# One unit of the next-to-last feed-forward job moved behind the last step of a two-layer recurrent transformer kernel

## The chip, the cores and the metric

The kernel runs on one core of one Trainium2 chip. The metric is the device time of one execution in microseconds (us). Engines are named as in the profile: PE is TensorE's matmul, PEld its weight load, DVE VectorE, ACT ScalarE, POOL GpSimd, SP SyncE, which issues most of the DMAs.

## The reference

Two layers over the same weights. Each layer is an attention block whose segments are chained by a memory, and a gated feed-forward block. All inputs are bf16; S = 2048 tokens, D = 576, 32 heads of 128, segments of 32 tokens, a memory of 8 tokens, F = 4608.

```python
def attention(x, mem, Wq, Wk, Wv, Wo):           # x: (1, 2048, 576)
    for s in range(64):                           # segments of 32 tokens
        h = concatenate([mem, x[:, 32*s:32*s+32]])          # 40 rows
        q, k, v = (einsum('btd,dhe->bhte', h, W) for W in (Wq, Wk, Wv))
        p = softmax(where(mask, q @ k.T * 128**-0.5, -1e9))
        o = einsum('bhte,hed->btd', p @ v, Wo)
        mem = o[:, :8]                            # the next segment needs it
        outs.append(o[:, 8:])
    return concatenate(outs)
def feed_forward(x, w1, w3, w2):
    return (silu(x @ w1) * (x @ w3)) @ w2

x = A_x
for _ in range(2):
    x = x + attention(layernorm(x), A_mem0, Wq, Wk, Wv, Wo)
    x = x + feed_forward(layernorm(x), w1, w3, w2)
```

## The kernel before

**Steps.** The memory chains the segments, so the kernel walks through them in 72 steps: in step t it computes segment t of the first layer (t below 64) and segment t - 8 of the second (t from 8 on). In steps 8 to 63 both layers' 40 rows go through the same matmuls as 80 columns; from step 64 on only the second layer is left. A step has eight groups of Q/K projections (letters Q for the full 128-row part, q for the 64-row rest), four of scores (S), transposes of the probabilities (T on TensorE where one layer is left, a DMA transpose into PTS where there are two), P x V (P), output projections (O, o), and V projections (V, v, X, x or G, g).

**Jobs.** After every fourth step 128 finished tokens of each layer go to a feed-forward job: POST (p) transposes them back and adds them to the residual XR, a layer norm follows on DVE and POOL, its transposes (n) go to PSUM, and `xtb_write` copies them into the tile XTB, 128 columns for each of the job's two groups of tokens (`bi`, the half). Then come nine units (`pp`), each with two pairs of up matmuls (`ffn_up`: F the full part, f the 64-row rest, 2 x 128 features of w1 and of w3), tanh on ACT, two multiplications on DVE into HTT, and then down matmuls (`ffn_down`, W or w) whose result two DVE instructions add to XR. The up weights of a pair (W13, four DMAs) have two slots, the down weights (W2C, one DMA a pair) two, so a load waits until an earlier unit's matmuls have freed its slot.

**The end.** Job 16 (group 14 of the second layer) runs beside steps 68 to 71, job 17 (group 15) after step 71. Each has one group of 128 tokens. Job 17 finds the weights of unit 8 still in the W13 and W2C slots, where job 16 leaves them (`kept`). For units 0 to 7 the attention weights are no longer needed: four chunks of up weights (1024 features, 2.4 MB each) are loaded into the tile W, and four of down weights (1.2 MB each) into WV (`tail_load`). An up chunk waits for the Q/K projections of step 71 that read its columns, a down chunk for that step's V projections (`last_reads`). Units 0 and 1 use chunk 0, units 2 and 3 chunk 1, and so on. Ahead of job 17's transposes, `ln_tr` issues ten matmuls on data that nothing reads (`warm`).

**Order.** `make_nodes` makes a list of nodes, each with its engine, an estimated duration, its dependencies and the slots that it takes and frees. The order on TensorE is written out as letters: `ORDER = FIRST + FOUR * 11 + LAST`, where FIRST covers steps 0 to 15, each FOUR four steps, and LAST steps 60 to 71. Nodes of a kind are taken in the order in which they were made. `plan` runs through that list with the estimated times and puts the other engines' nodes, SP's DMAs among them, in the order of the earliest planned start, by `prio` among those that could start; a node marked AD goes to ACT or DVE, whichever could start it first. Each engine then executes its list in order. All helpers record under one line each: L594 the matmuls, L597 ACT, L600 DVE, L603 SP's loads and stores, L1024 the DMA transposes, L1015 POOL's clearing of PB.

Of the kernel before, what the change touches and what calls it, by code (L numbers as in the profile page):

```python
# [7 lines left out]
BF = mybir.dt.bfloat16  # L8
# [187 lines left out]
def ewh(*ns):  # L196
# [15 lines left out]
    "vQQQQqfqWSFSFfqqqQQwWQFPfqfSFwQOPSWFoFPffOOWPwOoooFqqfQQWQSqqqQQaSbQQqgqqGSQgPGSGPGggOPOwOPoooOo"  # L212
)
LAST = (
    "QqqqpQQQSnpQQqqqVvSSnQFqfFqPfQOwSPWfFPOOoFfooFPWOoFffqqQQwQSFffqqFQQQgqqwWSGSQPFQqfgqGSWFPGfggGPOOOPwOooooFqqfqQ"
    "QQQfqWSFSvQQqqVwSFqfqQPQFSWPwOOPffFOWPwOooooFfqqQQQQqfqWSwVSFFvfqqQQQqqSPQWSOPVvPwOObPoooxOoXVppvqqQQQSqqQQqqnnS"
    "QQFTSqfQPqFSTOfPFTOPWTOPwOooooFqffqQQQSQqqVvSFTQqfqQQSFqfqwPQWTOSPFTOffPFTOPwOWooooFfqqQQQwSQqqfvxXVWSFFQfqqTQPw"
    "WTFSQQffqqFPSOTwWFPffOTFPWOOwooooFvqqfQQQSwQqqVSWFQfqfqFQQSTWPQqqOTSPoTOPwOToboPxOoXqqqQQQpSvVqqqQQnSQFSfTQFqqfP"
    "QOSTFfPowTOPfFTOPFOooowQqqfqQFSQQvqqfVSQFfqQQTSFqfqwPQTFPSOTXfxPOTOPwOooooFVvqfQQqqQSQqqqfQSQFTSQPqqQwOFToSfPFTO"
    "fPwTOPFOooofQQqqqqQSQQSvqqQVwTQSQqfqfPSTOPoFOTFPTOPwOooopfFFfnwFffffFFFwFfFwffFFwfffFFwFwfffFFFwffFFwfffFFww"  # L220
)
ORDER = FIRST + FOUR * 11 + LAST

# [5 lines left out]
    ustep, mode_pen, hor, wait, bulk, ff_split, last_win, tail_at = 0.0315, 0.1194, 0.0162, 0.141, 0.02, False, 2.5, -1.5  # L229


def make_nodes(em, nseg, pools, o=Opt, dma_bw=230e3, load_bw=400e3):

    ngrp = nseg // 4
    nodes = []
# [20 lines left out]
    def load(name, nbytes, prio, fn, deps=()):  # L256
        return node("DMA", nbytes / load_bw, fn, deps=deps, prio=prio, name=name, lat=2.0)
# [97 lines left out]
    def step(t):  # L355
# [17 lines left out]
        for g in range(NG):  # L373
# [79 lines left out]
    last_up = []  # L453
    last_reads = [], []
    kept = {}

    def job(j):

        ents = [(0, j)] if 0 <= j < ngrp else []
        if 0 <= j - 2 < ngrp:  # L460
            ents.append((1, j - 2))
# [8 lines left out]
        for (bi, g) in reversed(ents):  # L470
            pa = post(bi, g)
            wr += ln_nodes("F", xr[g], Slot("xn"), [pa], s0, [((lambda bi: lambda b: em.xtb_write(bi, b))(bi), cost, prev_ff)], last)
        mm = (128 * ne / 2.4 + 2.5) / 1000
        w2_last = {}
        tail = None
        if last:
            v_done, qk_done = last_reads
            tail = []
            for i in range(4):
                parts = [(0, 9 * 1024, qk_done[4 * i:4 * i + 4]), (1, 8 * 576, v_done)]  # L480
                tail += [[load("tail", kb(128, c), s0 + o.tail_at + 0.01 * i, em.tail_load(i, what), deps=dep) for what, c, dep in parts]] * 2

        npp = NPR // 2
        for at, pp in enumerate([npp - 1] + list(range(npp - 1)) if last else range(npp)):
            mids, w2s, htts, lds = [], [], [], []
            stays = last and pp == npp - 1
            for pr_ in (2 * pp, 2 * pp + 1):
                prio = s0 + o.ff + (o.win if s0 + 4 < nst else o.last_win) * (2 * at + pr_ % 2) / NPR
                if stays:
                    w13, w2 = kept[pr_]  # L490
                    ld = []
                    w2s.append(w2)
                elif last:
                    w13 = w2 = None
                    ld = tail[pp]
                else:
                    keep = s0 < nst <= s0 + 4 and pp == npp - 1
                    w13, w2 = Slot("w13", users=2 + keep), Slot("w2", users=ne + keep)
                    kept[pr_] = w13, w2
                    ld = [node("DMA", kb(1152, 256) / dma_bw, em.load_w13(pr_, w13), prio=prio - 1, acq=[w13], lat=2.0, name="W13")]  # L500
                    lds.append(node("DMA", kb(256, 576) / dma_bw, em.load_w2(pr_, w2), prio=prio - 0.99, acq=[w2], lat=2.0, name="W2l"))
                    w2s.append(w2)
                b = banks()
                htt = Slot("htt", users=ne)
                rel13 = [w13] if w13 else []
                fm = node("PE", 16 * mm, em.ffn_up(ents, pr_, w13, b, last and not stays, False), deps=wr + ld, prio=prio, mode="full/col",
                          acq=b + [htt], rel=rel13, name="FF")
                ff = node("PE", 2 * mm, em.ffn_up(ents, pr_, w13, b, last and not stays, True), deps=wr + ld, prio=prio + o.fft, mode="row",
                          acq=b + [htt], rel=rel13, name="FFt")
                a = node("ACT", actc(256 * ne), em.ffn_tanh(ents, b, htt), deps=[fm, ff], prio=prio - 0.5, name="tanh")  # L510
                c = node("DVE", 2 * dve(256 * ne) + 0.13, em.ffn_mul(ents, b, htt), deps=[a], prio=prio - 0.5, rel=b, name="mul")
                last_up[:] = [fm, ff]
                mids.append(c)
                htts.append(htt)
            for (bi, g) in ents:
                b = banks()
                d = node("PE", 8 * 0.1225, em.ffn_down(bi, pp, htts, w2s, b, last and not stays), deps=mids + lds, prio=prio + o.w2,
                         mode="full/col", acq=b, rel=htts + w2s, name="W2b" if bi else "W2")
                es = [node("DVE", dve(288), em.ffn_add(g, h, xr[g], b[h]), deps=[d], prio=prio + o.w2, rel=[b[h]], name="W2a")
                      for h in (0, 1)]  # L520
                w2_last[bi] = es
        for (bi, g) in ents:
            if bi == 0:
                ht_set(1, g, ln_nodes("L1", xr[g], Slot("xn"), w2_last[0], s0 + LAG - 4.2, ht_writes(1, g)))
            else:
                xn = Slot("xn")
                c = node("ACT", actc(576), em.fin_cast(xr[g], xn), deps=w2_last[1], prio=s0 + LAG - 4.2, acq=[xn], rel=[xr[g]], name="fin")
                node("SWD", 1.0, em.store(g, xn, last), deps=[c], prio=s0 + LAG - 4.2, rel=[xn], lat=3.0, name="store")

    def x_in(g):  # L530
        xn = Slot("xn")
# [39 lines left out]
class Emitter:  # L571
# [574 lines left out]


    def span(self, ents):
        bis = [bi for bi, _ in ents]
        return min(bis) * P, (max(bis) + 1) * P  # L1150

    def ffn_up(self, ents, pr, w13, b, last, tail):

        def f(n):
            lo, hi = self.span(ents)
            W = self.tail_w[pr][0] if last else self.T.W13[:, w13.i]
            first = self.begin(b)
            for fb in range(2):
                fs = slice(fb * P, (fb + 1) * P)
                os_ = slice(fb * 2 * P + lo, fb * 2 * P + hi)  # L1160
                for r in (0, 1):
                    if tail:
                        rr = slice(r * R64, (r + 1) * R64)
                        self.mm(self.bk(b[r])[:, os_], W[rr, 8, fs], self.T.XTB[rr, 4, lo:hi], first and fb == 0, fb == 1,
                                tile_position=(r * R64, 0))
# [52 lines left out]
def kernel(  # L1218
# [62 lines left out]
    T.M0 = T.XTB[:].rearrange("p a b -> p (a b)")[:, 0:D]  # L1281

    T.banks = [pp.tile([P, 512], F32, name=f"bank{i}") for i in range(pools["bank"])]

# [59 lines left out]
```

## Time and profile before

| What | Value |
|---|---|
| median of 3 runs | 2660.19 us (2660.15 to 2664.9) |
| profiled execution | 2656.83 us |
| its span, first to last instruction | 2654.8 us, mean granted clock 0.994 |
| PE busy | 2575.9 us, 97% of the span |
| DVE, ACT busy | 77%, 46% |
| chain that ended last | PE 83%, DMA 8%, DVE 5% |
| DMA | 373.21 MB, mean 141 GB/s |

The profile is of one execution; the times stated from it are us after its first instruction. Busy times of PE are modelled at the matmuls' ends. "PE <- X" in a list of waits is idle time of TensorE that X ended; "issue" is idle time that no semaphore ended. SPq rows are the times that SP took to issue a DMA, not its transfer. Step 71 begins at 2578.9 us, its POST matmuls (after the wait for YTS) at 2608.2, and the last store is issued at 2651.5.

### The profile page before, as it was taken

The numbers are of one execution on the slowest core, as the hardware profiler recorded it, in microseconds if no ns is written. First come the engines' busy times: TensorE is split into PE (matmuls) and PEld (weight loads), VectorE is DVE, ScalarE is ACT, GpSimd is POOL, SyncE is SP. The second block draws the span as 40 slices with busy tenths as digits, with TensorE's granted clock in tenths as the row PEclk, the third lists the DMA queues.
The fourth block names the chain that finished last, engine by engine and source line by source line (L and its number), as shares of the span: only waits on it lengthen the run. The fifth ranks groups of instructions, "written<-read, shape, count | busy, mean of one in ns | idle before, by whom it ended". The sixth has DMA issues, their size and how long they took to land.

```text
span 2654.8 us, 132820 instructions
## 1 busy us (share of the span) xinstructions
PE 2575.9 (97%) x58915; PEld 2224.6 (84%) x58915; DVE 2040.2 (77%) x5241; ACT 1229.2 (46%) x3648; POOL 334.7 (13%) x399
## 2 busy tenths in 40 slices
PE   5999999999999999999999999999999999999998
PEld 4788888888888888888888888888888887888876
DVE  4787777787787777877778787778877877877766
ACT  2555454444445444444445444454544434454553
POOL 1111110110111011010101111010111101111110
PEclk8999999999999999999999999999999999999999
DMA  9064845565565546456554655545455565544466
GB/s 322 4 185 122 195 107 142 123 147 138 126 153 116 136 118 165 126 135 165 109 132 116 153 135 134 157 119 140 109 141 143 126 156 107 136 116 137 130 181 222
DMA packets 686033, 373.21 MB, mean 141 GB/s; under 512 B 233896, under 2 KB 675632, under 8 KB 684816
## 3 DMA queue, kind: packets, MB, share of 16 engines
q1 hardware_dynamic: 681920, 356.84, 53.3%
q8 instruction: 460, 7.54, 1.2%
q0 software_dynamic: 3024, 6.93, 0.9%
q10 hardware_dynamic: 512, 0.94, 0.2%
q14 instruction: 117, 0.96, 0.1%
HBM read 308.49 MB, written 2.36 MB: 117 GB/s over the span
## 4 chain that ended last, share of the span: by engine, by line
PE 83%; DMA 8%; DVE 5%; SPq 2%; ACT 1%; issue 1%; POOL 0%; ACTq 0%; DVEq 0%; POOLq 0%
PE bank L594 83%; DMA PTS<-PB 5%; SPq L603 1%; DVE STAT L600 1%; DVE V L600 1%; DVE HTT L600 1%; DVE PB L600 1%; DMA W<-in_B_w_dram 1%; DMA W<-in_A_Wk_dram 1%; DVE SME L600 1%; ACT V L597 1%; DMA WV<-in_A_Wv_dram 0%; DVE XR L600 0%; DMA W2C<-in_B_w_dram 0%; POOL PB L1015 0%
## 5 line engine op out<-in xcount | busy, mean ns | idle before, releaser
L594 PEld LDWEIGHTS <-W 128*128 128x128 bf16 (+2 forms) x31824 | 1253.7, 100 | 138.5 <-issue 66.4
L594 PE MATMUL bank<-HT,W 128*128 128x80 bf16 (+3 forms) x23040 | 803.2, 197 | 20.6 <-DMA W<-in_A_Wk_dram 8.7
L594 PE MATMUL bank<-XTB,W 128*64 128x256 bf16 (+5 forms) x8784 | 666.6, 263 | 5.8 <-DMA W<-in_B_w_dram 5.5
L1015 POOL MEMSET PB<- 128x1024 bf16 x288 | 273.9, 951 | 1949.4 <-DMA PTS<-PB 1294.9
L597 ACT ACTIVATE QKT<-bank 128x256 bf16<-128x256 f32 (+4 forms) x1557 | 358.8, 315 | 303.9 <-PE bank L594 295.3
L594 PE MATMUL bank<-OT,WO 128*128 128x80 bf16 (+3 forms) x11520 | 412.1, 198 | 1.1 <-ACT OT L597 0.6
L594 PEld LDWEIGHTS <-WO 128*128 128x128 bf16 (+1 forms) x11520 | 383.7, 102 | 25.9 <-issue 13.5
L597 ACT ACTIVATE V<-bank 64x512 bf16<-64x512 f32 (+1 forms) x582 | 328.6, 584 | 127.3 <-PE bank L594 120.1
L594 PE MATMUL bank<-WV,HT 128*64 128x512 bf16 (+3 forms) x3960 | 376.0, 386 | 1.1 <-DVE HT L600 0.7
L594 PE MATMUL bank<-W2C,HTT 128*64 128x288 bf16 (+1 forms) x3088 | 320.0, 287 | 0.7 <-DMA W2C<-in_B_w_dram 0.5
L597 ACT ACTIVATE HTT<-bank 128x512 bf16<-128x512 f32 (+1 forms) x324 | 175.9, 551 | 273.4 <-PE bank L594 271.8
L600 DVE TENSOR_REDUCE STAT<-SME 104x8 f32<-104x320 f32 (+1 forms) x576 | 273.5, 475 | 16.9 <-ACT SME L597 10.5
L597 ACT ACTIVATE OT<-bank 128x320 bf16<-128x320 f32 (+1 forms) x380 | 142.8, 402 | 306.3 <-PE bank L594 304.2
L600 DVE TENSOR_TENSOR PB<-SME,STAT 40x128 bf16<-40x128 f32 (+4 forms) x912 | 275.1, 336 | 10.9 <-DVE STAT L600 0.7
L594 PEld LDWEIGHTS <-HT 128*64 128x64 bf16 (+3 forms) x3960 | 168.5, 102 | 116.3 <-issue 21.4
L600 DVE SCALAR_TENSOR_TENSOR HTT<-HTT,bank 128x512 bf16<-128x512 bf16 (+1 forms) x324 | 202.1, 624 | 82.7 <-ACT HTT L597 79.4
L600 DVE SCALAR_TENSOR_TENSOR XR<-bank,XR 128x288 f32<-128x288 f32 x576 | 245.0, 448 | 21.4 <-PE bank L594 16.5
L594 PEld LDWEIGHTS <-HTT 128*64 128x64 bf16 (+1 forms) x3152 | 228.0, 105 | 37.7 <-issue 3.1
L600 DVE TENSOR_TENSOR HTT<-HTT,bank 128x512 bf16<-128x512 bf16 (+1 forms) x324 | 203.6, 628 | 31.2 <-PE bank L594 0.9
L600 DVE CAST V<-bank 32x512 bf16<-32x512 f32 (+1 forms) x282 | 192.8, 684 | 39.2 <-PE bank L594 33.5
L597 ACT ACTIVATE SME<-SME 104x320 f32<-104x320 f32 (+1 forms) x288 | 135.1, 469 | 152.1 <-DVE SME L600 150.6
L600 DVE CAST QKT<-bank 128x192 bf16<-128x192 f32 (+2 forms) x491 | 133.3, 315 | 71.3 <-PE bank L594 69.5
(58 smaller groups left out, 1420.2 us busy)
## 6 DMA issues: line engine op xcount, KB each, us to landing
W<-in_B_w_dram SPq DMA_DIRECT2D x612, 256.0 KB, 3.7
W2C<-in_B_w_dram SPq DMA_DIRECT2D x306, 288.0 KB, 3.4
W<-in_B_w_dram SPq DMA_DIRECT2D x612, 32.0 KB, 3.8
W<-in_B_w_dram SPq DMA_DIRECT2D x8, 1024.0 KB, 13.2
W<-in_A_Wq_dram SPq DMA_DIRECT2D x9, 512.0 KB, 9.5
WO<-in_A_Wo_dram SPq DMA_DIRECT2D x4, 1152.0 KB, 16.6
XR<-in_A_x_dram POOLq DMA_DIRECT2D x16, 288.0 KB, 3.7
WV<-in_B_w_dram SPq DMA_DIRECT2D x4, 1152.0 KB, 12.4
```

Of the source, the lines that this page charges most:

```text
L594: self.ch("PE", self.nc.tensor.matmul(out, lhsT=lhsT, rhs=rhs, start=start, stop=stop, skip_group_check=True, **k))
L597: self.ch("ACT", self.nc.scalar.activation(*a, **k))
L600: self.ch("DVE", getattr(self.nc.vector, fn_)(*a, **k))
L603: self.ch("SP", self.nc.sync.dma_start(out=out, in_=in_))
L1015: return lambda n: self.ch("POOL", self.nc.gpsimd.memset(self.T.PB[:, pb.i], 0.0))
```

## The change

Unit 0 of job 16 leaves steps 68 to 71. Job 16 runs units 1 to 8 there and keeps unit 8's weights for job 17, as before. Unit 0 is made after job 17's tail loads (`rest`, called through `shared`), between job 17's POST and its transposes, and reads chunk 0 of the tail weights, which job 17's unit 0 reads again; its own four W13 loads per pair and its two W2C loads are gone. The cast and the store of group 14 follow it. The two jobs now use different halves of XTB (job 16 half 1, job 17 half 0), so job 17's write to XTB does not wait for job 16's last up matmuls (`prev_ff`), and XTB is laid out by halves, [2, 5, 128] instead of [5, 256]; a job with two groups reads its 256 columns as two runs of 128. `ents` carries the half beside the layer and the group. The letters of LAST are new, with the same number of each letter; FIRST and FOUR stay. Two figures of the planner change: the rate of the large loads (345 instead of 400 bytes per ns) and the DMA transpose (1.27 us with 2.0 us of latency instead of 1.25 and 1.7).

```diff
 LAST = (
...
-    "fPwTOPFOOofQQqqqqQSQQSvqqQVwTQSQqfqfPSTOPoFOTFPTOPwOooopfFFfnwFffffFFFwFfFwffFFwfffFFwFwfffFFFwffFFwfffFFww"
+    "FPwTOPoofOoFQQvqqQSQQqqVSQqqqQqQSTQPTSPFOOTffooPFTOPwOoopFffFwnwFffffFFFwFwfffFFFwfffFFwFwfffFFFwffFFwfffFFww"
...
-def make_nodes(em, nseg, pools, o=Opt, dma_bw=230e3, load_bw=400e3):
+def make_nodes(em, nseg, pools, o=Opt, dma_bw=230e3, load_bw=345e3):
...
-                tr = node("DMA", 1.25, em.ptr_dma(t, g, pb, pts), deps=[pbs], prio=pf - 0.02, acq=[pts], name="TR", lat=1.7)
+                tr = node("DMA", 1.27, em.ptr_dma(t, g, pb, pts), deps=[pbs], prio=pf - 0.02, acq=[pts], name="TR", lat=2.0)
...
+        before_last = s0 < nst <= s0 + 4
+        if last:
+            ents = [(bi, g, 0) for bi, g, _ in ents]
         wr = []
-        prev_ff = list(last_up)
+        prev_ff = [] if last else list(last_up)
...
+        def units(pps, at0, end):
+            for at, pp in enumerate(pps, at0):
+                mids, w2s, htts, lds = [], [], [], []
+                stays = last and pp == npp - 1
+                in_tail = end and not stays
...
+                    elif in_tail:
+                        w13 = w2 = None
+                        ld = tail[pp]
...
+        if last:
+            units([npp - 1] + list(range(npp - 1)), 0, True)
+        elif before_last:
+            units(range(1, npp), 0, False)
+
+            def rest():
+                units((0,), npp - 1, True)
+                finish()
+            shared.append(rest)
+            return
+        else:
+            units(range(npp), 0, False)
+        finish()
...
     def xtb_write(self, bi, b):
-        return lambda n: self.cp(n, self.T.XTB[:, :, bi * P:(bi + 1) * P], self.lnps(b))
+        return lambda n: self.cp(n, self.T.XTB[:, bi], self.lnps(b))
...
-                            self.mm(self.bk(b[r])[:, os_], W[:, 4 * r + c, fs], self.T.XTB[:, c, lo:hi], first and fb == 0 and c == 0,
+                            self.mm(self.bk(b[r])[:, os_], W[:, 4 * r + c, fs], self.T.XTB[:, lo // P:hi // P, c, :], first and fb == 0 and c == 0,
                                     fb == 1 and c == 3)
...
-    T.XTB = sp.tile([P, 5, 2 * P], BF, name="XTB")
+    T.XTB = sp.tile([P, 2, 5, P], BF, name="XTB")
```

More of the change, by code (lines that the diff above doesn't have):

```diff
@@ L474, in job, with norm @@
         w2_last = {}
[L475 removed]
+        npp = NPR // 2
+        def norm():
+            for (bi, g, half) in reversed(ents):
+                pa = post(bi, g)
+                wr.extend(ln_nodes("F", xr[g], Slot("xn"), [pa], s0, [((lambda half: lambda b: em.xtb_write(half, b))(half), cost, prev_ff)], last))
+        def units(pps, at0, end):
[3 more added lines that the diff above has]
+                in_tail = end and not stays
+                for pr_ in (2 * pp, 2 * pp + 1):
+                    prio = (s0 + 4 if end and not last else s0) + o.ff + (o.win if s0 + 4 < nst else o.last_win) * (2 * at + pr_ % 2) / NPR
+                    if stays:
+                        w13, w2 = kept[pr_]
+                        ld = []
+                        w2s.append(w2)
+                    elif in_tail:
+                        w13 = w2 = None
+                        ld = tail[pp]
+                    else:
+                        keep = before_last and pp == npp - 1
+                        w13, w2 = Slot("w13", users=2 + keep), Slot("w2", users=ne + keep)
+                        kept[pr_] = w13, w2
+                        ld = [node("DMA", kb(1152, 256) / dma_bw, em.load_w13(pr_, w13), prio=prio - 1, acq=[w13], lat=2.0, name="W13")]
+                        lds.append(node("DMA", kb(256, 576) / dma_bw, em.load_w2(pr_, w2), prio=prio - 0.99, acq=[w2], lat=2.0, name="W2l"))
+                        w2s.append(w2)
+                    b = banks()
+                    htt = Slot("htt", users=ne)
+                    rel13 = [w13] if w13 else []
+                    fm = node("PE", 16 * mm, em.ffn_up(ents, pr_, w13, b, in_tail, False), deps=wr + ld, prio=prio, mode="full/col",
+                              acq=b + [htt], rel=rel13, name="FF")
+                    ff = node("PE", 2 * mm, em.ffn_up(ents, pr_, w13, b, in_tail, True), deps=wr + ld, prio=prio + o.fft, mode="row",
+                              acq=b + [htt], rel=rel13, name="FFt")
+                    a = node("ACT", actc(256 * ne), em.ffn_tanh(ents, b, htt), deps=[fm, ff], prio=prio - 0.5, name="tanh")
+                    c = node("DVE", 2 * dve(256 * ne) + 0.13, em.ffn_mul(ents, b, htt), deps=[a], prio=prio - 0.5, rel=b, name="mul")
+                    last_up[:] = [fm, ff]
+                    mids.append(c)
+                    htts.append(htt)
+                for (bi, g, half) in ents:
+                    b = banks()
+                    d = node("PE", 8 * 0.1225, em.ffn_down(half, pp, htts, w2s, b, in_tail), deps=mids + lds, prio=prio + o.w2,
+                             mode="full/col", acq=b, rel=htts + w2s, name="W2b" if bi else "W2")
+                    es = [node("DVE", dve(288), em.ffn_add(g, h, xr[g], b[h]), deps=[d], prio=prio + o.w2, rel=[b[h]], name="W2a")
+                          for h in (0, 1)]
+                    w2_last[bi] = es
@@ new lines, in finish @@
+        def finish():
+            for (bi, g, half) in ents:
+                if bi == 0:
+                    ht_set(1, g, ln_nodes("L1", xr[g], Slot("xn"), w2_last[0], s0 + LAG - 4.2, ht_writes(1, g)))
+                else:
+                    xn = Slot("xn")
+                    c = node("ACT", actc(576), em.fin_cast(xr[g], xn), deps=w2_last[1], prio=s0 + LAG - 4.2, acq=[xn], rel=[xr[g]], name="fin")
+                    node("SWD", 1.0, em.store(g, xn, last), deps=[c], prio=s0 + LAG - 4.2, rel=[xn], lat=3.0, name="store")
@@ L476, in job @@
         if last:
             v_done, qk_done = last_reads
-            tail = []
             for i in range(4):
                 parts = [(0, 9 * 1024, qk_done[4 * i:4 * i + 4]), (1, 8 * 576, v_done)]
[L481 to L528, printed above, removed]
+                tail.extend([[load("tail", kb(128, c), s0 + o.tail_at + 0.01 * i, em.tail_load(i, what), deps=dep) for what, c, dep in parts]] * 2)
@@ L1148, in span @@
     def span(self, ents):
-        bis = [bi for bi, _ in ents]
+        bis = [half for _, _, half in ents]
         return min(bis) * P, (max(bis) + 1) * P
```

28 lines of the change are left out of this document (15 added, 13 removed).

## The prediction

> **What bounds the kernel now.** I read the page, then who TensorE waits for by stretch, then the end of the run on TensorE and on the queue that issues the loads. First the page:
>
> ```profile
> PE 2575.9 (97%) x58915; PEld 2224.6 (84%) x58915; DVE 2040.2 (77%) x5241; ACT 1229.2 (46%) x3648; POOL 334.7 (13%) x399
> PEclk8999999999999999999999999999999999999999
> ```
>
> TensorE is busy 97% of the span, at full clock in all but the first slice. The change neither adds nor removes a matmul, so only TensorE's idle time and half-clock time can move. The waits of TensorE, 120 to 2560 us (first line), then 2560 us to the end:
>
> ```profile
> PE bank L594 <- DMA PTS<-PB: 18.9, 29, 1.4
> ...
> PE bank L594 <- DMA W<-in_B_w_dram: 5.0, 1, 5.0
> PE bank L594 <- issue: 3.5, 2, 2.9
> PE bank L594 <- DVE YTS L600: 0.8, 1, 0.8
> ```
>
> The long middle holds 32 us of idle time in 2440 (windows: 2408.2 busy), mostly waits for transposes. The last 95 us hold two single gaps. The timeline of TensorE shows both (start, length, what; the bracket is the idle time before):
>
> ```profile
> 2584.76 0.35 PE L594 MATMUL bank<-QKT 128*40 128x40 bf16 x7
> 2588.02 0.22 PE L594 MATMUL bank<-QKT 128*40 128x40 bf16 x1 [2.91 <-issue]
> ...
> 2635.41 0.28 PE L594 MATMUL bank<-XTB,W 64*128 64x128 bf16 x4
> 2640.69 4.10 PE L594 MATMUL bank<-XTB,W 64*128 64x128 bf16 x36 [4.99 <-DMA W<-in_B_w_dram]
> 2644.62 1.14 PE L594 MATMUL bank<-WV,HTT 128*128 128x288 bf16 x8
> 2645.70 2.40 PE L594 MATMUL bank<-XTB,W 64*128 64x128 bf16 x44
> ```
>
> Gap 1 lies inside the scores of step 71 and ends for no semaphore. Gap 2 is the last job waiting for the last chunk of its weights. Each costs more than its length: the granted clock is one half from 2586.5 to 2593.3 and from 2637.7 to 2644.5. Behind gap 2, 36 matmuls take 4.10 us where 44 of the same kind then take 2.40, so 4.10 - 36/44 x 2.40 = 2.1 us are lost: gap 2 costs 4.99 + 2.1 = 7.1 us. Behind gap 1, 5.3 us run at half clock, 2.65 lost: 5.6 us in all.
>
> Why the last chunk is late stands in SP's timeline (start, issue time, what):
>
> ```profile
> 2594.55 0.89 SPq L603 DMA_DIRECT2D W2C<-in_B_w_dram  x2
> 2601.08 5.80 SPq L603 DMA_DIRECT2D W<-in_B_w_dram  x8
> 2606.99 1.04 SPq L603 DMA_DIRECT2D W2C<-in_B_w_dram  x2
> 2608.08 1.08 SPq L603 DMA_DIRECT2D WV<-in_B_w_dram  x2
> 2609.21 8.78 SPq L603 DMA_DIRECT2D W<-in_B_w_dram  x4
> ```
>
> and in the windows beside it (length; busy PE, PEld, DVE, ACT, POOL; clock, DMA share, GB/s):
>
> ```profile
> 2597.00:2601.00 4.00, 3.99 (x133) 3.54 (x131) 3.83 (x11) 2.72 (x11) 0.95 (x1) 1.00 0.31 91
> 2601.00:2609.00 8.00, 7.22 (x203) 6.43 (x198) 4.87 (x15) 2.99 (x11) 1.90 (x2) 1.00 0.62 174
> 2609.00:2630.00 21.00, 21.00 (x344) 17.92 (x343) 15.76 (x40) 5.94 (x14) 1.13 (x2) 1.00 1.03 334
> ```
>
> SP issues in order. At 2595 it stands before the up weights of unit 8 of job 16 (x8: eight loads), whose slots come free only when unit 7's up matmuls have run, at 2601. So the DMA engines idle (91 GB/s), then move unit 8's 1.77 MB (two pairs of 2 x 256 + 2 x 32 + 288 KB) in small rows, and the big tail loads behind them (WV from 2608.08) run at 334 GB/s until the last lands at 2640.6.
>
> **The change, part by part.** *The moved unit.* By the letters, job 16 in steps 68 to 71 now runs units 1 to 8 where units 0 to 7 ran, and unit 0 takes the place that unit 8 had, after step 71's POST. Before step 71 the same seven up units run, so it starts at the same time; one W2 group (1.14 us) leaves it and stands ahead of the last transposes instead: sum zero. Matmuls, DVE and ACT work: unchanged.
>
> *Loads removed.* Ten issues (about 0.5 us each on SP, which is not the bound there) and 1.77 MB. What stands behind them on SP are the tail loads. Unit 8's up weights now stand where unit 7's stood (before 2579), so WV's first chunks can go once step 71's V matmuls are done (2593.6 now). That is 2597 instead of 2608.1. From the first WV issue to the last landing took 32.5 us: it now ends at about 2630, or, with the two W2C loads of unit 8 between (0.59 MB at 334 GB/s, 1.8 us), 2632. TensorE gets to that chunk at 2635.7, where gap 2 begins. If SP instead met those W2C loads ahead of WV, it would stand until unit 7's W2 is done (2606 now, 2605 then): 2605 + 1.8 + 32.5 = 2639, and 4 us of gap 2 would stay. I take the first: WV needs only the V matmuls, and the planner takes what is ready first. Gap 2 goes: -7.1 us. Next in line is then TensorE itself, which has 3 us in hand.
>
> *A new short wait.* Unit 8's W2 matmuls now run right behind unit 0's up matmuls, about 2610; their W2C load waits for unit 7's W2 (2605) and lands 3.5 us after its issue by the median, 4.3 for the pair at 2594.55 under load: 2609.3. Behind that W2 on TensorE queue the warm-up matmuls, the last job's transposes and everything else. Bounds 0 to 4 us; I take +0.8, nearer to the margin of zero.
>
> *XTB by halves.* The last job writes its own half and no longer waits for job 16's last up matmuls; before, those ended at 2611 and the transposes at 2613.6, so nothing is won. The wide up matmuls now read two runs of 128 columns instead of one of 256. P x V reads two runs of 40 already; the groups by shape:
>
> ```profile
> L594 PE MATMUL bank<-HT,W 128*128 128x80 bf16 x14336 | 557.4, 202 | 5.0 <-ACT HT L597 4.4 <-issue 0.5
> ...
> L594 PE MATMUL bank<-PTS,V 128*128 128x80 bf16 x1192 | 67.6, 202 | 17.5 <-DMA PTS<-PB 16.0 <-DVE PB L600 1.2
> ```
>
> 202 ns either way, so 0, with rounding of 0.5 ns over 5040 matmuls as the bound: 2.5 us either way.
>
> *New letters for steps 60 to 71.* By the planner's modes they have 209 changes of tile mode instead of 218. In the trace a change spaces two starts 131 ns where 36 is usual: 9 x 0.095 = -0.9 us.
>
> *Planner's figures* (transpose 1.27 + 2.0 us instead of 1.25 + 1.7; tail loads at 345). The order on TensorE is written out and stays until step 59, but DVE's, ACT's and SP's order follows planned times. Measured, a transpose takes 3.1 us from issue to landing by the median, so the plan comes nearer to the chip. No row prices the reshuffle: between winning and losing half of the 18.9 us, +-9; I take 0. The store of group 14 moves behind unit 0, thirty us before the end: nothing.
>
> Sum: -7.1 + 0.8 - 0.9 = -7.2 us. The profiled execution took 2656.83 us (span 2654.8 and 2.0 around it), so 2649.6; the median shown, 2660.19, is 3.4 higher, and on it the forecast is 2653.0.
>
> **Gap 1 and the rules.** Why I leave it: the code of TensorE comes in blocks of 16 KB for 256 instructions (460 of them, 117,760 instructions). A block's transfer usually starts when 215 instructions past the previous mark have started; the one at 2585.58 starts at 449, the latest of the run, 5 us after the first tail loads fill the queues. So TensorE ran out of code behind bulk loads, and the new kernel sends the same bulk at the same point. [...]
>
> **The rivals.**
> 1. Gap 1 goes too, because the block falls due at another point: -7.2 - 5.6 = -12.8, 2647.4 us. For it: one late block among three in that stretch. Against: the load now runs without pause from 2581 to 2602. Chance 0.15.
> 2. The gain is given back at the end: unit 8's W2C late by 4 us, a second code stall (2.9 and half clock, 5), or SP's order as above. It leaves -1 to -4: 2656 to 2659 us. Chance 0.20.
> 3. Slower, by the transposes of steps 8 to 63. They share SP's queue with the up weights; planned 0.3 us later, one can come to stand behind a load of four issues (2 us). A late transpose now costs 18.9/29 = 0.65 us, and the written pattern of four steps repeats eleven times. One more late transpose per pattern costs 7.2 and cancels the gain; two cost 14.4: +7.2, 2667 us. For it: 77% busy DVE and 29 waits show little slack. Against: of 224 transposes TensorE now waits visibly for 29. Chance 0.15.
>
> **The numbers.** The forecast has 0.50. A measurement of this kernel can tell about 0.2%, 5.3 us, from no change. The forecast's own spread (1 to 3 us) puts some 0.10 of it within that; so faster 0.40 + 0.15 = 0.55, same 0.10 + 0.20 = 0.30, slower 0.15. The range takes in rival 1 and 2 us beyond (2645) and reaches up to two thirds of the way to rival 3 (2664).
>
> **What would show it.** In the new profile: no wait of TensorE for W in the last 60 us and no half clock at 2637; WV issued on SP before 2600; unit 8's W2C near 2605 and its wait under 2 us; a gap of about 3 us by "issue" in step 71 again; waits for transposes between 120 and 2560 us near 19. A wait for W that stays over 4 us, or waits for transposes over 26, would make the prediction wrong.

## The result and the profile after

The changed kernel took 2656.62 us (median of 13 runs, 2650.5 to 2660.16) beside 2661.94 us (13 runs, 2657.12 to 2665.75) of the kernel before: a ratio of 0.9975, 95% interval 0.9966 to 0.9983. On 2661.94 us that is 6.6 us won (4.5 to 9.0; the two medians alone differ by 5.3), where 7.2 were forecast.

The page of the changed kernel, its lines for TensorE and for the granted clock:

```profile
PE 2577.3 (97%) x58915; PEld 2226.7 (84%) x58915; DVE 2042.0 (77%) x5253; ACT 1226.3 (46%) x3636; POOL 334.9 (13%) x399
PEclk8999999999999999999999999999999999999999
```

The matmuls are as many as before, and the 1.77 MB are gone from the reads (306.72 MB from HBM; 308.49 before). The two profiled executions themselves hardly differ, 2657.08 and 2656.83 us, and hide the gain: step 59 ends at 2219.8 us instead of 2211.7. Those 8 us are the spread between executions and no work of the change, so I compare times within an execution. The output of step 59 came at 2217.9 to 2228.6 us in nine profiles that have the new kernel's lists up to there, and at 2211.7, 2220.9, 2226.0, 2226.9 and 2226.9 in five with the old ones. From there on TensorE of the changed kernel is faster: 431.2 us from step 59's output to its last matmul, 438.5 before. I cut that stretch at the outputs of steps 70 and 71:

| stretch, us | before | after |
|---|---|---|
| step 59's output to step 70's | 367.1 | 364.2 |
| step 71 | 28.6 | 30.6 |
| step 71's output to the last matmul | 42.8 | 36.4 |
| idle by "issue" in the last 95 us | 3.5 (longest 2.91) | 6.1 (longest 2.90) |
| half clock in the last 95 us | 13.7 | 10.2 |

The waits of TensorE in the changed kernel, 120 to 2560 us (first line), then 2560 us to the end:

```profile
PE bank L620 <- DMA PTS<-PB: 19.9, 29, 1.5
...
PE bank L620 <- issue: 6.1, 3, 2.9
PE bank L620 <- DVE YTS L626: 0.8, 1, 0.8
```

The wait for W at the end is gone, and no wait for W2C took its place. The idle time without a semaphore has grown from 3.5 to 6.1 us. The timeline of TensorE (start, length, what; the idle time before in brackets) shows both:

```profile
2589.81 1.05 PE L620 MATMUL bank<-HT,W 128*128 128x40 bf16 x39 [1.36 <-issue]
...
2597.12 2.40 PE L620 MATMUL bank<-HT,W 64*128 64x40 bf16 x79 [2.90 <-issue]
...
2603.33 0.41 PE L620 MATMUL bank<-PTS,V 128*128 128x40 bf16 x7 [1.83 <-issue]
...
2617.89 1.34 PE L620 MATMUL bank<-W2C,HTT 128*64 128x288 bf16 x16
...
2643.27 2.29 PE L620 MATMUL bank<-XTB,W 64*128 64x128 bf16 x40
2645.40 1.14 PE L620 MATMUL bank<-WV,HTT 128*128 128x288 bf16 x8
2646.48 2.40 PE L620 MATMUL bank<-XTB,W 64*128 64x128 bf16 x44
```

Three gaps now lie in step 71, and one stretch of half clock around the last of them and behind it (2598.9 to 2609.1). At the end all runs at full clock: 40 matmuls in 2.29 us where 36 took 4.10. Now SP's timeline (start, issue time, what):

```profile
2591.64 0.37 SPq L629 DMA_DIRECT2D WV<-in_B_w_dram  x1
2592.06 6.74 SPq L629 DMA_DIRECT2D W<-in_B_w_dram  x4
2613.15 1.22 SPq L629 DMA_DIRECT2D W2C<-in_B_w_dram  x2
2614.43 1.13 SPq L629 DMA_DIRECT2D WV<-in_B_w_dram  x2
2615.60 6.52 SPq L629 DMA_DIRECT2D W<-in_B_w_dram  x4
```

and the windows beside it (length; busy PE, PEld, DVE, ACT, POOL; clock, DMA share, GB/s), step 71 first, a stretch inside it, and the stretch behind it last:

```profile
2584.00:2614.60 30.60, 24.50 (x719) 21.45 (x713) 17.58 (x49) 12.54 (x40) 3.80 (x4) 0.83 0.70 226
2606.00:2613.20 7.20, 7.20 (x214) 6.73 (x213) 4.90 (x16) 2.64 (x8) 1.90 (x2) 0.78 0.06 20
2614.60:2651.00 36.40, 35.63 (x591) 30.55 (x591) 27.54 (x68) 9.45 (x24) 1.13 (x2) 1.00 0.73 248
```

One WV chunk and up chunk 1 go out at 2592, and then SP stands before unit 8's W2C until unit 7's down matmuls are done, while the DMA engines idle (20 GB/s). The last chunk landed at about 2642, later than before (2640.6), but closer to step 70's output (58 us after it, 62 before). TensorE came to it only at 2643.3, a little over 1 us after it had landed.

### The profile page after: what moved, and what is told of

It is laid out like the page before. It is cut to its first block, busy times and chain, and to the rows that moved or that the text cites. A ratio compares the mean times of both kernels' runs of the same rounds, so it can differ in the third digit from the quotient of the medians.

```text
span 2655.3 us, 132788 instructions
## 1 busy us (share of the span) xinstructions
PE 2577.3 (97%) x58915; PEld 2226.7 (84%) x58915; DVE 2042.0 (77%) x5253; ACT 1226.3 (46%) x3636; POOL 334.9 (13%) x399
## 3 DMA queue, kind: packets, MB, share of 16 engines
q8 instruction: 460, 7.54, 1.2%
HBM read 306.72 MB, written 2.36 MB: 116 GB/s over the span
## 4 chain that ended last, share of the span: by engine, by line
PE 83%; DMA 8%; DVE 5%; issue 1%; ACT 1%; SPq 1%; POOL 0%; ACTq 0%; DVEq 0%; POOLq 0%
PE bank L620 83%; DMA PTS<-PB 6%; DVE V L626 1%; DVE STAT L626 1%; DMA W<-in_B_w_dram 1%; DVE HTT L626 1%; DVE PB L626 1%; DVE SME L626 1%; DMA W<-in_A_Wk_dram 1%; SPq L629 1%; DMA W2C<-in_B_w_dram 1%; POOL PB L1041 0%; DMA WV<-in_A_Wv_dram 0%; DVE XR L626 0%; ACT V L623 0%
## 5 line engine op out<-in xcount | busy, mean ns | idle before, releaser
L620 PE MATMUL bank<-WV,HT 128*32 128x512 bf16 (+3 forms) x3952 | 376.4, 386 | 1.2 <-DVE HT L626 0.7
L626 DVE TENSOR_REDUCE STAT<-SME 104x8 f32<-104x320 f32 (+1 forms) x576 | 273.6, 475 | 15.7 <-ACT SME L623 9.6
L620 PEld LDWEIGHTS <-HT 128*32 128x32 bf16 (+3 forms) x3952 | 168.3, 102 | 116.5 <-issue 22.1
L626 DVE CAST V<-bank 64x512 bf16<-64x512 f32 (+1 forms) x281 | 192.2, 684 | 42.7 <-PE bank L620 36.3
```

The lines of the kernel that those rows point to most:

```text
L620: self.ch("PE", self.nc.tensor.matmul(out, lhsT=lhsT, rhs=rhs, start=start, stop=stop, skip_group_check=True, **k))
L626: self.ch("DVE", getattr(self.nc.vector, fn_)(*a, **k))
```

## The experiments

Two questions were open: which of the edits removed gap 2, and what the gaps by "issue" in step 71 are. For the second I used the transfers of TensorE's code that the trace holds: 16 KB each, one for every 256 instructions (460 in either profile, before and after, 7.54 MB). I call one due when TensorE has started 215 instructions past the previous mark, which is about where it usually starts (the median is 215 in the kernel before and 218 in the changed one), and late by the time until it does. In the ratios below, each kernel stands against runs of the kernel before that were measured beside it. All runs, and the numbers that the verdicts rest on (us; "end" is from step 71's output to the last matmul; idle time by "issue", half clock and the waits for W and W2C over the last 95 us; "latest block" is the lateness of the latest code block in step 71):

```
                       ratio, 95% interval      step 71  end   issue  half   W,W2C waits  latest block
before                 1                        28.6     42.8  3.5    13.7   5.0          3.9
changed kernel         0.9975 [0.9966, 0.9983]  30.6     36.4  6.1    10.2   0            4.65
before, new figures    0.9985 [0.9974, 0.9996]  31.9     36.2  4.9    10.2   0            3.7
change, old figures    0.9980 [0.9971, 0.9990]  33.9     36.2  6.8    13.7   0            4.3
before, XTB by halves  1.0003 [0.9992, 1.0015]  28.5     42.9  3.1    13.7   4.8          3.8
before, no unit 8 load 0.9982 [0.9971, 0.9993]  31.1     37.1  8.0    3.4    0            4.2
change, no tail loads  0.9938 [0.9921, 0.9955]  24.0     36.2  1.5    0      0            1.4
change, 256 KB loads   0.9958 [0.9943, 0.9973]  28.6     36.2  4.0    6.8    0            3.3
change, W2 of 7 early  0.9990 [0.9976, 1.0004]  33.1     38.7  8.0    13.7   0            3.6
both of these          0.9966 [0.9953, 0.9979]  28.5     38.0  4.0    10.2   0            3.0
change, 128 KB         0.9987 [0.9974, 0.9999]  23.4     48.3  0.6    10.2   9.3          1.3
128 KB, W2 of 7 early  0.9985 [0.9974, 0.9997]  25.1     44.8  0.8    10.2   5.2          2.1
128 KB throughout      1.0010 [0.9998, 1.0023]  24.6     51.4  1.1    13.7   10.0         1.7
before, 128 KB         1.0011 [1.0001, 1.0022]  31.9     43.0  1.2    13.7   9.3          1.7
```

### Which edit removed gap 2

**The planner's two figures alone**, on the kernel before:

```diff
-def make_nodes(em, nseg, pools, o=Opt, dma_bw=230e3, load_bw=400e3):
+def make_nodes(em, nseg, pools, o=Opt, dma_bw=230e3, load_bw=345e3):
-                tr = node("DMA", 1.25, ..., name="TR", lat=1.7)
+                tr = node("DMA", 1.27, ..., name="TR", lat=2.0)
```

> The kernel before with the planner's two new figures alone (transpose 1.27 + 2.0 us, large loads at 345); letters, units and XTB as before. Theory A (the gain is made behind step 71, by the tail loads): the figures move hardly anything in the engines' lists, gap 2 stays (a wait for W of about 5 us near 2636 to 2641, half clock behind it), the time within 2 us of the kernel before. Theory B (the rival of the prediction: the reshuffled order of the transposes costs time in steps 8 to 63): slower by 4 to 7 us, waits for PTS between 120 and 2560 us over 24 us, step 59 reached 4 us later than in the kernel before.

It took 2668.23 us beside 2672.46, 0.15% faster, and its gap 2 is gone, although unit 8 is still loaded. SP's timeline of this kernel:

```profile
2605.83 0.37 SPq L603 DMA_DIRECT2D WV<-in_B_w_dram  x1
...
2609.15 0.89 SPq L603 DMA_DIRECT2D W2C<-in_B_w_dram  x2
2610.09 7.72 SPq L603 DMA_DIRECT2D W<-in_B_w_dram  x8
```

Theory A, by which gap 2 would stay, missed. The figures put one WV chunk (1.2 MB) ahead of unit 8's loads, into the time in which SP stood idle, and up chunk 1 right behind unit 8's first pair (both are in the x8 row at 2610.09). That is only part of why no wait for W is left. Counted from step 70's output the last chunk landed 60.5 us later, 62.1 before, so 1.6 us were won there; TensorE came to it at 60.0 us instead of 56.9, because step 71 took 31.9 us, with two gaps by "issue" of 2.6 and 2.2 us. No time is left over: the 40 matmuls there take 2.67 us where 2.29 are usual. So the larger part of gap 2 went because TensorE came later. The middle did not move: up to step 59 eight operations go to the other one of ACT and DVE and SP's list is the same, and TensorE waits 21.5 us for transposes (36 times), beside 21.1 us (32 times) in the next run, with the old figures on the same chip.

**The change with the old figures**, the reverse edit on the changed kernel:

```diff
-def make_nodes(em, nseg, pools, o=Opt, dma_bw=230e3, load_bw=345e3):
+def make_nodes(em, nseg, pools, o=Opt, dma_bw=230e3, load_bw=400e3):
-                tr = node("DMA", 1.27, ..., name="TR", lat=2.0)
+                tr = node("DMA", 1.25, ..., name="TR", lat=1.7)
```

> The changed kernel with the planner's old figures (1.25 + 1.7 us, 400). Theory A: as the changed kernel, 4 to 7 us faster than before, no wait for W behind step 71. One down chunk (WV) moves ahead of unit 8's W2C loads on SP, so the last tail load is issued about 3 us earlier. Theory B: faster than the changed kernel by 4 to 7 us, so 9 to 13 us faster than before.

2667.98 us, 0.20% faster: without the figures the moved unit removes gap 2 as well. Here the last chunk landed 59.1 us after step 70's output, and TensorE came to it at 62.5. With either of the two the wait is gone, and together they do not add: 0.15%, 0.20% and 0.25% have intervals that overlap.

**XTB by halves alone**, on the kernel before:

```diff
-        return lambda n: self.cp(n, self.T.XTB[:, :, bi * P:(bi + 1) * P], self.lnps(b))
+        return lambda n: self.cp(n, self.T.XTB[:, bi], self.lnps(b))
-    T.XTB = sp.tile([P, 5, 2 * P], BF, name="XTB")
+    T.XTB = sp.tile([P, 2, 5, P], BF, name="XTB")
```

> The kernel before with XTB laid out by halves and nothing else: the wide up matmuls read two runs of 128 columns. Theory A: two runs cost nothing, time within 1.5 us of before, mean of the 128x256 matmuls 273 ns as before, gap 2 stays. Rival: a few ns a matmul in 5040 matmuls, slower by 5 us or more, growing evenly over steps 12 to 67.

1.0003 (0.9992 to 1.0015). Its row of the wide up matmuls in the list of groups:

```profile
L594 PE MATMUL bank<-XTB,W 128*128 128x256 bf16 x1952 | 233.2, 273 | 0.1
```

273 ns, as in the kernel before (233.0 us in all): two runs of columns cost what one costs.

**The kernel before without unit 8's load in job 16** (unit 8 computes there, and in job 17, with weights that lie in the slots):

```diff
-                    ld = [node("DMA", ..., em.load_w13(pr_, w13), ...)]
+                    ld = [node("DMA", ..., (lambda n: None) if keep else em.load_w13(pr_, w13), ...)]
```

and the same for `load_w2`.

> The kernel before without the four up loads pairs and the W2C loads of unit 8 in job 16 (1.77 MB left out: unit 8 computes with the weights that lie in the slots). Order on TensorE, letters and figures as before. Theory A: SP no longer stands before these loads, WV is issued near 2597 instead of 2608, the wait for W at 2636 and the half clock behind it go: 6 to 8 us faster than before, as much as the change or a little more. Rival (gap 2 is made by the order on TensorE or by the rate of the loads, not by what stands ahead of them on SP): the gap stays over 3 us, gain under 3 us. By both, the gap by 'issue' in step 71 stays (3 to 6 us), since the tail loads still start there.

2668.41 us, 0.18% faster (4.8 us, where 6 to 8 were expected): no wait for W, an end of 37.1 us. WV's first chunk went out 15.7 us after step 70's output instead of 29.2, and the last load landed 47.6 us after it instead of 62.1. So it was unit 8's rows on SP that made the last chunk late, as the prediction read it; the run leaves out their 1.77 MB too, and doesn't tell SP's stand from the bytes. Yet TensorE now waits

```profile
PE bank L594 <- issue: 8.0, 6, 2.9
```

against 3.5 us before. SP issues loads from 2599.8 to 2605.2 us and without a pause from 2611.75 to 2635.35, and much of what was won at the end is lost again by these gaps, all but one of them (1.3 us) in step 71.

### What the gaps by "issue" are

**The changed kernel without the tail loads** (units 0 to 7 behind step 71 compute with the attention weights):

```diff
-            if what != 1:
+            if False:
...
-            if what != 0:
+            if False:
```

> The changed kernel with the tail loads left out (units 0 to 7 of the end compute with the attention weights that lie in W and WV); everything else, the order on TensorE too, unchanged. Theory C (the gaps by 'issue' in step 71 are TensorE out of code, because a block's transfer waits behind bulk loads): with no bulk beside step 71 the code blocks there start less than 1.2 us after they are due (3.5 to 4.6 us in the changed kernel), no gap by 'issue' over 0.6 us after step 70, no half clock before the last instruction, and the stretch from step 70's output to TensorE's end falls from 67 us to 55 to 58 us; time 12 to 16 us below the kernel before. Rival (the gaps belong to the code's place or to the scores themselves): gaps of 1.5 to 3 us stay in step 71, stretch 62 to 67 us.

0.62% faster than before. Its windows over step 71:

```profile
2591.40:2615.40 24.00, 22.36 (x719) 19.46 (x713) 17.39 (x49) 11.98 (x39) 3.81 (x4) 1.00 0.16 45
```

The same 719 matmuls take 24.0 us instead of 30.6, at full clock. Of the 6.6 us, 4.5 are less idle time (30.6 - 24.5 = 6.1; 24.0 - 22.4 = 1.6) and 2.1 are the half clock (24.50 - 22.36 busy). Small gaps stay:

```profile
PE bank L620 <- issue: 1.5, 2, 0.9
```

so the expectation (no gap over 0.6 us, 55 to 58 us from step 70's output to the end) was not quite met: that stretch took 60.3 us. Both gaps lie early in step 71. The code block due at 2593.5, beside the last of unit 8's small loads (254 GB/s until 2595), is 1.4 us late; the later blocks, beside 5 to 14 GB/s, are 0.3 to 0.6 us late and leave no gap. In the changed kernel, beside the loads, one is 4.65 and one 3.5 us late.

The instruction counts settle what the gaps are. In all fourteen profiles, the 30 gaps by "issue" of half a us or more in the last 95 us begin at one and the same place within the 256 instructions of a block (remainder 193; 174 or 175 in the traces that lack some 19 matmul records), and each ends 1.25 to 1.64 us after the last byte of a code block has come. The latest block starts at instruction 449 past the mark in six of these profiles, the kernel before and the changed one among them, and 449 is 193 + 256. So TensorE stops where it has used up the code that it holds and goes on when the next block is there: the gaps are TensorE without code. That they are long beside the bulk loads and short or gone without them shows that the loads make them.

**Smaller loads.** The 1 MB up loads in four of 256 KB, the 1.2 MB down loads in four of 288 KB:

```diff
-                    self.dma(t13[:, 4*kind:4*kind+4], wd[0:4*P, fa:fa+1024].rearrange(...))
+                    for c in range(4):
+                        self.dma(t13[:, 4*kind+c], wd[c*P:(c+1)*P, fa:fa+1024])
-                self.dma(t2, ...)
+                for b in range(0, 8, 2):
+                    self.dma(t2[:, b:b+2], self.a.w2[fa+b*P:fa+(b+2)*P, :].rearrange("(b p) d -> p b d", p=P))
```

> The changed kernel with each 1 MB up load of the tail cut into four DMAs of 256 KB (rows of 2 KB as before) and each 1.2 MB down load into four of 288 KB; same bytes, same order. Theory C1 (a code block's transfer waits for whole DMAs ahead of it, so its lateness goes with the size of one DMA): blocks in step 71 start 0.6 to 1.5 us late instead of 3.5 to 4.6, the 'issue' gaps fall from 6 us to under 2, half clock goes, 4 to 8 us faster than the changed kernel. Theory C2 (it waits for the bytes queued, however they are cut): lateness 3 to 5 us as now, time within 1.5 us of the changed kernel.

2661.55 us beside 2672.11, 0.42% faster. Theory C1 expected under 2 us by "issue" and no half clock, C2 no change; the run lies between them. Its waits and windows (step 71, and 16 us inside it):

```profile
PE bank L620 <- issue: 4.0, 3, 2.2
```

```profile
2586.40:2615.10 28.70, 24.63 (x721) 20.97 (x715) 17.54 (x49) 12.37 (x41) 3.80 (x4) 0.88 0.77 248
2590.00:2606.00 16.00, 12.29 (x343) 9.77 (x339) 9.69 (x26) 8.52 (x28) 1.76 (x2) 0.89 1.01 323
```

Step 71 is 2 us shorter than in the changed kernel, the loads run at 323 GB/s inside it (329 there), and the end is 36.2 us (36.4 there). Of the versions that do the whole computation, this has the best ratio. Against the changed kernel, which was measured beside other runs of the kernel before (median 2661.94 us; 2672.11 here), the intervals overlap slightly, so that step rests on step 71's rows.

**Unit 7's down matmuls earlier.** SP stands before unit 8's W2C until they are done, so their letter moves forward, on the changed kernel and on the one with 256 KB loads:

```diff
-    "FPwTOPoofOoFQQvqqQSQqqVSQqqqQqQSTQPTSPFOOTffooPFTOPwOoopFffFwnwF...
+    "FPwTOPoofOoFQQvqqQSwQqqVSQqqqQqQSTQPTSPFOOTffooPFTOPOoopFffFwnwF...
```

> The changed kernel with one letter moved: the down matmuls of unit 7 stand behind the first scores of step 71 instead of behind its last P x V, so the slots of unit 8's W2C loads come free about 20 us earlier and SP does not stand before them. The tail loads then run on without the pause of 7 us (from 2606 to 2613 in the changed kernel's profile) and the last lands about 7 to 10 us earlier. By the prediction's own account (SP's order behind W2C) nothing waits for those loads any more, so the time is that of the changed kernel, within 1.5 us, the gaps by 'issue' stay. If the loads now also run beside the rest of step 71, Theory C expects one more late block there: up to 3 us slower.

> Both: loads cut as in the split kernel and unit 7's down matmuls early. Theory C1: no late blocks and no pause, 5 to 9 us faster than the changed kernel, the best of these four that computes everything. Theory C2: as the kernel with the one letter moved.

(The row with the minus is the changed kernel's; the row that the section on the change shows for these steps has one Q too many.)

0.9990 and 0.9966: neither is a gain on its parent. The first was expected within 1.5 us of the changed kernel or up to 3 us slower and came out 4.0 slower; the second was expected 5 to 9 us faster than it and came out 2.4 faster, and the intervals overlap in both. The first, meant to take the pause on SP away, has 8.0 us by "issue" and 13.7 us of half clock, five code blocks in a row 3.3 to 3.6 us late. With 256 KB loads it is 4.0 us by "issue", as on its parent.

**Pieces of 128 KB for the first two chunks** (144 KB for the down weights):

```diff
+                    for c in range(4):
+                        for s in (0, 512):
+                            self.dma(t13[:, 4*kind+c, s:s+512], wd[c*P:(c+1)*P, fa+s:fa+s+512])
...
+                for b in range(8):
+                    self.dma(t2[:, b], w2[fa+b*P:fa+(b+1)*P, :])
```

> The changed kernel with the loads of chunks 0 and 1, which run beside step 71, cut into pieces of 128 KB (rows of 1 KB) and 144 KB; the other chunks as before. SP needs about 0.4 us to issue one, so it hands out some 330 GB/s, less than the 380 to 400 that the big loads reach, and no queue builds up ahead of a code block. Theory C3 (the lateness of a block goes with the bytes queued ahead of it; cutting helps as far as SP's issue then holds the queue short): blocks in step 71 start 0.5 to 1.5 us late (1.1 to 3.3 when cut to 256 KB, 2.3 to 4.6 uncut), 'issue' gaps under 1.5 us in all, no half clock; from step 70's output to TensorE's end 61 to 63 us (64.9 when cut to 256 KB, 67.1 uncut); 3 us faster than the kernel cut to 256 KB. Rival (lateness depends on the share of the DMA engines in use alone): as the kernel cut to 256 KB, 64 to 66 us.

Waits, SP's timeline, and the windows over step 71 of this kernel:

```profile
PE bank L620 <- DMA W2C<-in_B_w_dram: 9.3, 2, 9.2
...
PE bank L620 <- issue: 0.6, 1, 0.6
```

```profile
2614.86 10.88 SPq L629 DMA_DIRECT2D W<-in_B_w_dram  x18
2626.15 0.90 SPq L629 DMA_DIRECT2D W2C<-in_B_w_dram  x2
```

```profile
2593.60:2617.00 23.40, 22.52 (x719) 19.31 (x713) 17.39 (x49) 12.10 (x40) 3.80 (x4) 1.00 0.69 201
```

Step 71 is as short as without the loads, at full clock, with code late by 0.6 to 1.3 us, although 201 GB/s flow beside it. But from step 70's output to the end it takes 71.7 us, where 61 to 63 were expected: I had not counted SP. An issue takes it 0.6 us (10.88/18), so 128 KB pieces pass at about 200 GB/s, and unit 8's W2C stands behind them until 2626.15, 10.5 us after unit 7's down matmuls had freed its slot (2615.6). The wait of 9.2 us and the half clock at the end (10.2 us, where none was expected) eat the gain.

Three variants follow from that: the earlier letter with it, all four chunks in 128 KB pieces with the earlier letter, and the 128 KB pieces for two chunks on the kernel before.

> The same with unit 7's down matmuls moved ahead in step 71, so that SP does not stand before unit 8's W2C loads. Theory C3: the big loads of chunks 2 and 3 now come into the second half of step 71 and make blocks late again there (2 to 3.5 us): 1 to 4 us slower than without the move. Rival (share alone): the same as without the move.

> As the run before, with all four chunks cut fine. Theory C3: no late block over 1.5 us in step 71, none of the late ones of the run before; the last load lands 47 to 52 us after step 70's output, just in time or up to 2 us late: end stretch 61 to 64 us. Rival (share alone): 65 to 67 us.

> The kernel before, nothing moved, with chunks 0 and 1 cut fine. Theory C3: the gap by 'issue' of 2.9 us in step 71 and its half clock shrink to under 1 us (up to 5 us won), gap 2 (the wait for W at the end, 4 to 5 us and half clock) stays or grows by what TensorE now comes earlier (5 to 10 us): time 0 to 3 us below the kernel before. So the moved unit and the cut loads are worth more together than the cut alone. Rival: cutting alone gives the kernel before as much as it gives the changed one (6 us or more).

0.9985, 1.0010 and 1.0011. Idle time by "issue" is 0.8 to 1.2 us in all three, on the kernel before too, where it was 3.5. The end is 45, 51 and 43 us, with 5.2, 10.0 and 9.3 us of waits for W and W2C over the last 95 us (5.7 of the 9.3 lie in step 71). The pieces cure the one and cause the other. None of the three came out as expected: the first is equal to the run before it (expected 1 to 4 us slower), the second takes 76.0 us from step 70's output to the end (expected 61 to 64), and the third is 0.11% slower than the kernel before (expected 0 to 3 us faster).

## Why the prediction was right

**Gap 2** was forecast at -7.1. The stretch behind step 71 shrank by 42.8 - 36.4 = 6.4 us, and it holds one down group (1.14 us) more, which came from step 71. So the work in that stretch got 7.5 us faster. In the run without unit 8's load, with the old letters, it takes 37.1 us, 1.3 of them a gap by "issue": 42.8 - 35.8 = 7.0 us for gap 2 itself, and some 0.5 for the new order. That term was right, and the cause of the late load too (the same run).

**The way to it** was not as told. The prediction took WV's chunks to follow freely from 2597 and the last to land at 2630 to 2632; it worked out, and set aside, that SP would stand before unit 8's W2C, with a landing at 2639 and 4 us of gap 2 left. SP did stand there, for 14.5 us, behind one WV chunk and one up chunk. Only one WV chunk of four went out before 2600, and W2C went out at 2613 instead of 2605. Counted from step 70's output, the last chunk landed at 58.2 us where it had landed at 62.1, so 3.9 us earlier, and TensorE came to it at 59.3 us instead of 56.9, so 2.4 us later. The margin of 3 us that the prediction had for its free path is a little over 1 us.

Why did the branch that was set aside leave no wait? From the issue of unit 8's W2C to the last landing it had 1.8 + 32.5 = 34.3 us; measured were 29.0. One WV chunk had gone ahead, 1.2 MB, worth 3.5 us at 334 GB/s; the rest is priced by no run. And a longer step 71 does not by itself make a margin: SP goes on when unit 7's down matmuls, in step 71, are done, and from these TensorE needs 30 us to the last chunk (29.6 before, 29.9 now). The kernel with 256 KB loads has a step 71 of 28.6 us and no wait either. "The planner takes what is ready first" was too short a reason: it does so by its own times, and those put the W2C slot free earlier than the chip did.

**Gap 1 "stays"** is the term that was mis-sized. The cause that the prediction named is shown: code behind bulk loads. Its price was nearer to 5.0 than to 5.6, since the half clock behind it cost 2.1 us (the three groups take 5.65 us; 3.59 in the run without tail loads). But the same bulk did not meet the same code. Counted from step 70's output, the first two up chunks went out after 1.7 and 5.1 us in the kernel before; now they go out after 2.6 and 8.1 us, with a WV chunk after 7.7 just ahead of the second. Four blocks in a row are now 2.3, 4.65, 3.5 and 1.7 us late. Before, three were late by 3.9, 3.6 and 1.1 us, and the second of these cost no gap: TensorE was in the V projections, of which 32 matmuls last 3.39 us. Idle time by "issue" grew from 3.5 to 6.1 us. Step 71 became 2.0 us longer although a down group (1.14 us) left it; only 0.6 us of work came in, a part of a 128-row up group that fell before step 70's output until now. So 2.0 + 1.1 - 0.6 = 2.5 us were given back, as much as the idle time by "issue" grew (2.6); the half clock costs 2.1 us in both. That is the second code stall of rival 2, in step 71 instead of at the end, and smaller than its 5 us. Rival 1 did not come.

Where next to nothing is loaded, in the later part of step 71 in the run without tail loads (5 to 14 GB/s), the blocks are 0.3 to 0.6 us late and leave no gap. Beside the loads step 71 takes 6.6 us more (30.6 us instead of 24.0).

**New letters** were priced at -0.9. From step 59's output to step 70's, nine profiles with the new letters take 366.2 us in the mean (364.2 to 369.5), five with the old ones 369.2 (367.1 to 370.9). Of the 3.0, 0.6 is the part of the up group that now falls into step 71; 2.4 remain, and 2.3 in the two traces of the table (367.1 - 364.2 - 0.6). Each set scatters by 4 to 5 us, so the size is rough, and all nine also have the moved unit: that the letters alone do it is not shown.

**The wait for W2C** (+0.8) was about 0.2, without slack: the second load of the pair was issued at 2613.62 and landed at about 2618.2, and the group that needs it began at 2617.9 and took 1.34 us where the same sixteen matmuls took 1.15 before. **XTB by halves** is 0, as taken. **The planner's figures** are 0 in the middle (step 59's output comes at 2222.7 us in the mean of the nine profiles with the new lists, at 2222.5 in the five with the old), and rival 3 falls: 19.9 us of waits for transposes, 29 of them as before. At the end they were not nothing, since alone they end the wait for W, if in part by a longer step 71; the prediction looked for their effect only in steps 8 to 63.

Sum: -7.5 behind step 71, +2.5 in it, -2.3 ahead of it: -7.3 us, which is what the two traces show from step 59's output to the last matmul (431.2 - 438.5; the parts are cut from it, so they must add up to it). The ratio gives -6.6 (-9.0 to -4.5). The mechanism of the main term was right, but that the forecast of -7.2 came so close is in part luck, through errors that cancel: the code stalls gave back 2.5 us that it did not count, the stretch behind step 71 (-7.1 + 0.8 in the forecast) came out better by 1.2, and the letters by 1.4.

## What to carry to other kernels

An idle gap that no semaphore ends, in dense small matmuls (here 40 columns, some 25 to 30 ns each: 112 in 3.12 us, 79 in 2.05), beside bulk loads, is worth a look at when the engine's own code arrived: moving the loads earlier or closer together can turn a wait for data into a wait for code (in the kernel before without unit 8's load, the wait for W went from 5.0 us to 0 and the idle time by "issue" from 3.5 to 8.0). Pull a load away from dense code, or cut it, before making it earlier (in the changed kernel the idle time by "issue" fell from 6.1 us to 4.0 with 256 KB loads). And when loads share an in-order queue, as SP's is here, follow each queue entry to what it waits for on the real times: a small load that waits for a slot holds all behind it (14.5 us in the changed kernel), and small pieces in front of it hold it (10.5 us with 128 KB pieces).

## What I had not expected of the hardware

Where the loads beside step 71 come in 1 MB transfers, code blocks are up to 4.65 us late, at 256 KB up to 3.3, at 128 KB up to 1.3 us (1.7 to 2.1 in the three variants), and without them up to 0.6 (1.4 beside unit 8's small loads). Smaller pieces also made the loads slower (329, 323 and 201 GB/s), so the runs do not separate the size of one transfer from the bytes queued at a time.

A row of 2 KB of the loads takes 0.084 us in the median of the changed kernel's trace, so 4.65 us are, by estimate, the time of 55 such rows on one DMA engine (4.65/0.084). The traces do not tell what holds the block back in the queues; that stays open. A kernel that cuts the loads only while step 71 runs and issues unit 8's W2C ahead of the pieces was not tried.

The stretches at half clock in the last 95 us, up to the last matmul, are 3.4, 6.8 or 10.2 us long each (6.83 and 6.83 in the kernel before, 10.24 in the changed one, none in the run without tail loads), so here they come in units of 3.4 us. Idle gaps of 1.36, 2.90 and 1.83 us, none of them as long as that, came with three such units in step 71 of the changed kernel, and 6.1 us of idle time there cost 8.2 with the 2.1 us of the half clock.
